# A batch's first layer as one full-precision product instead of three rounded ones, the gate of a convolution in one operation, and a new order

## The chip, the core and the metric

The kernel runs on one core of a Trainium2 chip. A core has a matrix engine (TensorE, PE in the profile; its weight loads are listed as PEld), three engines for elementwise work (VectorE or DVE, ScalarE or ACT, GpSimd or POOL), and SyncE (SP), whose queue issues nearly all of this program's DMAs. Each engine works through its own instructions in the order in which the program lists them, and engines wait for each other by semaphores. Operands lie in an on-chip memory of 128 partitions (SBUF); PE writes its products to eight accumulator banks (PSUM). The metric is the device time of one execution in microseconds.

## The reference, cut to what matters

```python
B, H, S, D = 4, 8, 576, 64                 # batches, heads, positions, head size
def attention(q, k, v):                    # windowed: 32 keys back; heads 4 to 7 with a step of 4
    scores = where(mask[h], q @ k.T / sqrt(D), -1e9)
    return softmax(scores) @ v             # joined over heads: x, (B, S, 512)

def gated_mlp(x, w_in, conv_w, w_out):     # w_in (512, 1024), w_out (1024, 512)
    h = maximum(x @ w_in, 0)               # the first layer
    conv = conv_w[0] * h[s - 1] + conv_w[1] * h[s] + conv_w[2] * h[s + 1]   # over positions
    return (h * sigmoid(conv)) @ w_out     # the second layer

def mixing(x, w_ch1, w_ch2):               # w_ch1 (512, 2048), w_ch2 (2048, 512)
    u = x + real(fft(fft(x, axis=1), axis=2))
    return u + maximum(normalize(u) @ w_ch1, 0) @ w_ch2
```

The weights arrive as 64-bit floats, and everything is wanted in 32-bit precision.

## The kernel before

**Precision by parts.** A product whose operands are rounded to a shorter mantissa (type fp32r in the listing) is one pass on PE. `mm3` makes a product of nearly full precision out of three: each operand is split into a high part (rounded) and a low part (the remainder), and high x high, high x low and low x high are added up in one bank. A split is a rounding copy on ScalarE or GpSimd and a subtraction (`lo_of`) on DVE. `mm` with plain fp32 operands is a full-precision product; the attention scores and the products with the values use it. In a trace a full fp32 product stands as two records.

**Stages.** The attention of a batch comes as 14 ticks (`tick`): scores by PE, a maximum over the keys by a GpSimd reduction, a subtraction on DVE, an exponential on ScalarE, the product with the values, a normalization, and a turn on PE that brings the result to x's layout (`xT[b]`: 128 partitions by four chunks of 576 positions, with a high and a low part). Batch b's gated MLP runs while the ticks of batch b + 1 are worked off. It goes over eight blocks of 128 features: `m1(b, f)` multiplies the first layer (two halves of 288 positions, four chunks, three passes: twelve products a half), takes ReLU into a padded row buffer `hpad`, makes the three taps of the convolution, tanh and the gate, and splits the gated result into `gh` and `gl`; `m2(b, f)` multiplies it by the second layer into banks 4 to 7 (four groups of three products of 512 columns). The gate is made in two operations, since the second half of the positions is stored back to front. After eight blocks `evac` copies the sums out and `fold` adds and subtracts mirrored positions for the Fourier transform, whose tables and products (`dft`), the normalization (`ln`) and the last MLP follow and take the rest of the time.

**Weights.** `Weights.convert` brings one tile of 128 x 512 raw 64-bit weights by DMA into one of two buffers (`raw`). Three integer operations on DVE (`narrow`) turn it into fp32 in place, and `split` makes the two parts that `mm3` needs. First-layer tiles (`W1.tiles[0, f]`) and second-layer tiles (`W1.tiles[1, f]`) of the gated MLP are made during batch 0 and stay for all four batches.

**What sets the order.** Nothing is issued while the code is recorded. `Plan` notes each operation with its reads, writes, an estimated duration per engine that may take it, and a due time. `order` then plays the engines forward and takes for each the ready work that is due first. Due times come from `T0`, `PER` (the period of a batch) and `WHEN`; `urgency` carries them back to what a work needs, and `NUDGES`, a list of random seeds, shifts the due times of works in random stretches of the plan. Where the plan finds PE idle for more than 0.4 us, `fill` puts in products of the identity matrix (`busy_with`, line 1277), called fillers here, which compute nothing that is used.

## Time and profile before

| | us |
|---|---|
| median of 3 runs | 738.28 |
| lowest, highest | 736.79, 740.48 |
| the profiled execution | 739.48 |
| its span, first instruction to last | 737.7 |

The profile is that of one execution. A row of a group gives how many instructions of one kind ran, how long they kept their engine, the mean duration of one, and the engine's idle time before them with what ended it. Products on PE overlap: the duration of one is longer than the distance from its start to the next one's start, so prices for PE are read from starts in the listing by time. In that listing (rows 5) consecutive equal products are merged into one row. Stages are cut here where PE starts the first product of a batch's first layer: at 40.0, 111.8, 189.3 and 248.4 us.

### The profile page before, as it was taken

How to read it: one execution, taken by the hardware profiler on the slowest of the kernel's cores; microseconds unless marked ns; L12 is line 12 of the kernel's file. 1: busy time of each engine (PE TensorE's matmuls, PEld its weight loads, DVE VectorE, ACT ScalarE, POOL GpSimd, SP SyncE). 2: the span in 40 equal slices, each digit the busy share in tenths (PEclk: the TensorE clock that was granted, in tenths of full speed). 3: DMA queues.
4: the chain of work that ended last, by engine and by line, in shares of the span. 5: the costliest groups of instructions: out<-in, count | busy, mean ns of one | idle time of the engine just before them, and what ended most of it. 6: DMA issues, size and time to landing. Idle time of an engine off the chain costs nothing.

```text
span 737.7 us, 12036 instructions
## 1 busy us (share of the span) xinstructions
PE 723.6 (98%) x4264; PEld 641.2 (87%) x4264; DVE 558.1 (76%) x1157; ACT 342.7 (46%) x874; POOL 156.5 (21%) x171
## 2 busy tenths in 40 slices
PE   7999999999999999999999999999999999999997
PEld 5888889998999999888798888898889889888896
DVE  5899999999998689999887988676788648324223
ACT  3876767776676665454333325233333323222211
POOL 5766425542554122120100100000010000000000
PEclk9999999999999999999999999999999999999999
DMA  8754444324600825687976813034456799546202
GB/s 284 236 170 129 157 133 154 118 79 133 205 23 1 282 88 185 203 297 244 342 242 203 283 57 115 29 142 129 143 185 235 244 366 367 150 121 228 87 1 87
DMA packets 75184, 126.85 MB, mean 172 GB/s; under 512 B 7594, under 2 KB 36010, under 8 KB 74484
## 3 DMA queue, kind: packets, MB, share of 16 engines
q1 hardware_dynamic: 74324, 123.13, 50.9%
q0 software_dynamic: 432, 2.67, 1.1%
q8 instruction: 34, 0.56, 0.3%
q10 hardware_dynamic: 368, 0.28, 0.1%
q14 instruction: 26, 0.21, 0.1%
HBM read 90.11 MB, written 35.94 MB: 171 GB/s over the span
## 4 chain that ended last, share of the span: by engine, by line
PE 84%; DVE 8%; DMA 4%; POOL 1%; issue 1%; SPq 1%; ACT 0%; ACTq 0%; DVEq 0%; POOLq 0%
PE pb L274 84%; DVE win L261 2%; DMA raw<-in_wm_dram 2%; DVE rows L261 2%; DVE wf L261 1%; POOL mx L261 1%; DMA unt<-nd 1%; DVE raw L261 1%; DMA cst<-in_conv_dram 1%; SPq L307 1%; DVE sm L261 1%; DMA maskt<-in_mask_dram 1%; DVE x L261 0%; POOL wf L261 0%; DVE hid L261 0%
## 5 line engine op out<-in xcount | busy, mean ns | idle before, releaser
L274 PE MATMUL pb<-wf,hid 128*128 128x512 f32 x870 | 229.8, 398 | 0.0
L274 PEld LDWEIGHTS pb<-wf,hid 128*128 128x128 f32 x870 | 157.0, 188 | 25.8 <-DVE hid L261 0.3
L274 PE MATMUL pb<-x,wf 128*128 128x288 f32 x768 | 116.1, 299 | 1.7 <-DVE wf L261 1.5
L274 PEld LDWEIGHTS pb<-x,wf 128*128 128x128 f32 x768 | 106.2, 188 | 4.9 <-DVE wf L261 2.5
L261 POOL PARTITION_ALL_REDUCE mx<-sm x56 | 86.5, 1558 | 59.7 <-DVE sm L261 28.4
L274 PE MATMUL pb<-wf,wc 128*128 128x384 f32 (+1 forms) x414 | 85.3, 343 | 0.0
L274 PEld LDWEIGHTS pb<-wf,wc 128*128 128x128 f32 x414 | 74.2, 188 | 6.0
L261 DVE TENSOR_TENSOR work<-pb,work 128x384 f32<-128x384 f32 x48 | 26.6, 555 | 64.0 <-ACT work L261 35.6
L261 ACT COPY work<-pb 128x384 f32<-128x384 f32 x48 | 23.0, 479 | 82.9 <-PE pb L274 82.9
L261 DVE SCALAR_TENSOR_TENSOR rows<-rows,convw 128x576 f32<-128x576 f32 x64 | 55.8, 872 | 3.6 <-ACT rows L261 2.9
L274 PE MATMUL pb<-wf 128*128 128x512 f32 x216 | 55.3, 393 | 0.0
L274 PEld LDWEIGHTS pb<-wf 128*128 128x128 f32 x216 | 40.1, 188 | 6.5
L673 ACT ACTIVATE xb<-pb,rs 72x64 f32<-72x64 f32 (+1 forms) x184 | 41.6, 305 | 7.8 <-DVE rs L261 7.7
L274 PEld LDWEIGHTS pb<-VT,sm 104*72 104x72 f32 (+1 forms) x448 | 39.4, 153 | 4.7 <-ACT sm L261 2.6
L274 PE MATMUL pb<-VT,sm 104*72 104x65 f32 (+1 forms) x448 | 41.2, 236 | 1.5 <-ACT sm L261 1.4
L274 PE MATMUL pb<-QT,KT 128*104 128x144 f32 (+1 forms) x224 | 41.0, 305 | 0.7 <-DMA QT<-in_qt_dram 0.7
L274 PE MATMUL pb<-wf,wf 128*128 128x512 f32 (+1 forms) x162 | 40.3, 385 | 0.0
L261 ACT ACTIVATE rows<-pb 128x288 f32<-128x288 f32 x64 | 26.5, 414 | 28.2 <-PE pb L274 27.9
L274 PEld LDWEIGHTS pb<-QT,KT 128*104 128x104 f32 (+1 forms) x224 | 33.2, 178 | 5.8 <-issue 3.8
L261 ACT ACTIVATE hid<-pb 128x512 fp32r<-128x512 f32 (+1 forms) x32 | 18.3, 572 | 35.9 <-PE pb L274 35.9
L274 PEld LDWEIGHTS pb<-wf,wf 128*128 128x128 f32 x162 | 30.0, 188 | 5.7
L274 PE MATMUL pb<-unt,wc 128*128 128x384 f32 x168 | 33.1, 335 | 0.0
(197 smaller groups left out, 1238.3 us busy)
## 6 DMA issues: line engine op xcount, KB each, us to landing
raw<-in_wm_dram SPq DMA_DIRECT2D x42, 512.0 KB, 4.9
wc<-cd SPq DMA_DIRECT2D x56, 256.0 KB, 3.5
cd<-wc SPq DMA_DIRECT2D x4, 1792.0 KB, 10.1
rows<-ud SPq DMA_DIRECT2D x20, 256.0 KB, 4.1
y<-yd SPq DMA_DIRECT2D x18, 256.0 KB, 4.3
ud<-y SPq DMA_DIRECT2D x18, 256.0 KB, 4.1
wf<-nd SPq DMA_DIRECT2D x18, 256.0 KB, 4.6
QT<-in_qt_dram SPq DMA_DIRECT2D x31, 144.0 KB, 3.5
```

Of the source, the lines that this page charges most:

```text
L261: getattr(self.engines[eng], name)(**a)
L274: getattr(self.engines["PE"], name)(*[v.real() for v in a], **kw)
L307: self.engines[eng].dma_start(out=out.real() if outs else out, in_=in_.real() if ins else in_)
L673: nc.scalar.mul(out=x[:, i], in_=p[:, i], mul=r[:, i:i + 1])
```

## The change

Batch 0's x is kept in fp32 alone (`x_first`, in space that the results of a batch use later), so a tick of batch 0 ends in one copy on ScalarE or DVE and no subtraction. Its first layer is multiplied by `mm` in full fp32: four products a half instead of twelve. For that the first-layer weights stay unsplit at first. `narrow` writes them to a small buffer (`ways`: three of them, in `e9` and `fs_t`), and a DMA brings them to their place; `later` splits them in place, block by block, when batch 1's turn comes. Each half now takes 290 columns instead of 288, two beyond its border, so that both halves lie in the row buffer with their own borders, the second one back to front from the start. The taps then run over both halves in one pattern of 2 x 289 elements, and the gate is one operation. A copy of one element sets the position that both halves share. The results of a batch (`y_t`, `o_t`, `e9`) become parts of one tile. `PER` and `NUDGES` change, and with them the order of the whole program.

```diff
-PER = 69.0
+PER = 68.0
-NUDGES = (8271, 49756, 57394, 51589, 33461, 98847, 32710, 84961, 42106, 40158, 90060, 79165,
+NUDGES = (55523, 99683, 99992, 79439, 80785, 13914, 19249, 38109, 26493, 77070, 73723, 9275,
...
-    rows_t = moe.tile([128, 4 * (S + 2)], F32, "rows")
-    hpad = [rows_t[:, i * (S + 2):(i + 1) * (S + 2)] for i in range(2)]
-    cv_t, g_t = (rows_t[:, i * (S + 2):i * (S + 2) + S] for i in (2, 3))
+    HW, GW = HS + 3, HS + 1
+    rows_t = moe.tile([128, 4 * HW + 4 * GW], F32, "rows")
+    hpad = [rows_t[:, 2 * HW * i:2 * HW * (i + 1)] for i in range(2)]
+    cv_t, g_t = (rows_t[:, 4 * HW + 2 * GW * i:4 * HW + 2 * GW * (i + 1)] for i in range(2))
...
-    y_t = [low.tile([128, DM], F32, "y") for _ in range(4)]
-    o_t = low.tile([128, DM], F32, "o")
-    e9 = low.tile([128, DM], F32, "e9")
+    y6 = low.tile([128, 6 * DM], F32, "y")
+    *y_t, o_t, e9 = (y6[:, DM * i:DM * i + DM] for i in range(6))
+
+    x_first = y6[:, 0:4 * S].rearrange("p (c s) -> p c s", c=4)
...
+    ways = Ring([e9, fs_t[:, 0:512].bitcast(F32), fs_t[:, 512:1024].bitcast(F32)])
...
             if load:
                 dma(raw, self.src[f, :, i])
-            self.split(w, raw)
+            if self.late and not i:
+                way = ways()
+                self.narrow(raw, way)
+                dma(w[:, 0].bitcast(F32), way)
+            else:
+                self.split(w, raw)
...
+        def later(self, f):
+
+            w = self.tiles[0, f]
+            w0 = w[:, 0].bitcast(F32)
+            copy(w[:, 1], w0, ("ACT", "POOL"))
+            lo_of(w[:, 0], w0, w[:, 1])
+            self.tiles[0, f] = w[:, 1::-1]
...
         x = xT[b][:, hp]
+        if not b:
+            x = x_first[:, hp]
+            if dil:
+                x = x.rearrange("p (m r) -> p m r", r=4)[:, :, t]
+            else:
+                x = x[:, 192 * t:192 * t + 192]
+            P.run({"ACT": 0.41 if dil else 0.32, "DVE": 0.42 if dil else 0.35}, "copy", at + 10, out=x, in_=bt)
+            return
...
+        def taps(at, row):
+            return rows_t[:, h0 + at:h0 + at + 2 * row].rearrange("p (t s) -> p t s", t=2)[:, :, :GW]
         for half in range(2):
-            o = of("h", h_banks)[:, :HS]
-            sl = slice(HS * half, HS * half + HS)
+            o = of("h", h_banks)[:, :HS + 2]
+            sl = slice(286 * half, 286 * half + HS + 2)
             with P.products(at + 4.3 * half):
                 for c in range(4):
                     wsl = slice(128 * c, 128 * c + 128)
-                    mm3(o, w[:, 0, wsl], w[:, 1, wsl], xT[b][:, c, 0, sl], xT[b][:, c, 1, sl], c == 0, c == 3)
-            P.run({"ACT": 0.41}, "activation", out=hp[:, 1 + HS * half:1 + HS * half + HS], in_=o, func=AF.Relu,
-                  scale=0.5)
...
+                    if b:
+                        mm3(o, w[:, 0, wsl], w[:, 1, wsl], xT[b][:, c, 0, sl], xT[b][:, c, 1, sl], c == 0, c == 3)
+                    else:
+                        mm(o, w[:, 0, wsl].bitcast(F32), x_first[:, c, sl], c == 0, c == 3)
+            P.run({"ACT": 0.41}, "activation", out=hp[:, HW + 2:] if half else hp[:, 1:HW],
+                  in_=o[:, HS + 1:0:-1] if half else o, func=AF.Relu, scale=0.5)
...
-        dve("scalar_tensor_tensor", 0.48, out=g[:, 0:289], in0=cv[:, 0:289], scalar=1.0, in1=hp[:, 1:290],
-            op0=ALU.add, op1=ALU.mult)
-        dve("scalar_tensor_tensor", 0.48, out=g[:, 289:576], in0=cv[:, 575:288:-1], scalar=1.0,
-            in1=hp[:, 576:289:-1], op0=ALU.add, op1=ALU.mult)
+        dve("scalar_tensor_tensor", 0.77, out=g, in0=cv, scalar=1.0, in1=taps(1, HW), op0=ALU.add, op1=ALU.mult)
+        P.run({"ACT": 0.2, "POOL": 0.3}, "copy", out=g[:, 1, 0:1], in_=g[:, 0, HS:GW])
...
             at = T0 + PER * b + step * f
+            if b == 1:
+                W1.later(f)
             m1(b, f, h_banks, at)
```

What the order becomes is shown at three places. In the listings `pb0` to `pb7` are the banks, a row with x12 stands for twelve equal instructions.

PE in batch 0's stage, before, from one half of feature block 1 to the next block's (`x_192` is batch 0's x, `wf4_152` the first-layer weights of blocks 0 to 3, `QT`/`KT` the scores, `VT` the product with the values, `ident`/`xb` the turn):

```order
L274 MATMUL pb0_134<-QT_203,KT_200 128x192 x2
L274 MATMUL pb2_136<-x_192,wf4_152 128x288 x12
L274 MATMUL pb3_137<-ident_145,xb_220 128x96 x2
L1277 LDWEIGHTS ident_145
L1277 MATMUL pb4_138<-ident_145 128x256
L274 MATMUL pb1_135<-VT_206,sm_210 96x65 x4
L274 MATMUL pb2_136<-x_192,wf4_152 128x288 x12
```

The same place after (`y_177` holds `x_first`):

```order
L273 MATMUL pb2_136<-y_177,wf4_152 128x290 x4
L273 LDWEIGHTS ident16_192
L273 MATMUL pb0_134<-maskt_191,ident16_192 128x384
L273 MATMUL pb0_134<-QT_198,KT_195 128x192 x2
L273 MATMUL pb2_136<-y_177,wf4_152 128x290 x4
L273 MATMUL pb1_135<-VT_201,sm_205 96x65 x4
L273 LDWEIGHTS ident16_192
L273 MATMUL pb0_134<-maskt_191,ident16_192 104x288
L273 MATMUL pb0_134<-QT_196,KT_193 104x144 x2
L273 MATMUL pb2_136<-y_177,wf4_152 128x290 x4
```

Twelve products became four, the filler is gone, and a tick's scores stand in its place; over the whole program there were 75 fillers and are 13 (six at the program's start, two more ahead of batch 0's first product, none in the stages of the MLP's first three batches, five later).

DVE around batch 0's first convolution (`rows<-rows,convw`), before: a first-layer weight tile is split right there (`wf4_152`), then a second-layer tile is narrowed (`win`, `raw`) and split (`wf_155`).

```order
L261 TENSOR_TENSOR wf4_152<-raw_161,wf4_152 128x512
L261 RECIPROCAL rs_216<-rs_216 96x4
L261 TENSOR_SCALAR win_163<-raw_162 128x512
L261 SCALAR_TENSOR_TENSOR win_163<-raw_162,win_163 128x512
L261 SCALAR_TENSOR_TENSOR raw_162<-raw_162,win_163 128x512
L261 SCALAR_TENSOR_TENSOR rows_169<-rows_169,convw_146 128x576 x2
L261 TENSOR_TENSOR x_167<-pb7_141,x_167 128x192
L261 RECIPROCAL rs_217<-rs_217 96x4
L261 TENSOR_TENSOR wf_155<-raw_162,wf_155 128x512
```

After:

```order
L260 TENSOR_TENSOR wf_155<-raw_162,wf_155 128x512
L260 TENSOR_TENSOR x_167<-pb6_140,x_167 128x192
L260 TENSOR_SCALAR win_163<-raw_161 128x512
L260 SCALAR_TENSOR_TENSOR win_163<-raw_161,win_163 128x512
L260 TENSOR_TENSOR x_167<-pb7_141,x_167 128x192
L260 SCALAR_TENSOR_TENSOR rows_169<-rows_169,convw_146 128x578 x2
L260 TENSOR_TENSOR x_167<-pb1_135,x_167 128x192
L260 SCALAR_TENSOR_TENSOR y_177<-raw_161,win_163 128x512
L260 SCALAR_TENSOR_TENSOR rows_169<-rows_169 128x578
```

The first-layer tile that is narrowed here (block 3's, into `y_177`, which is `e9`) has no split; the gate is one row (`rows_169<-rows_169 128x578`). Between the first convolutions of batch 0 and batch 1 DVE has 13 splits before and 8 after.

DVE around batch 0's last convolution, shortly before PE can reach batch 1's first product, after (`wf4_152<-wf4_152` is a split by `later`, `x_167` a low part of batch 1's x; the last of these stands in the third row):

```order
L260 TENSOR_TENSOR wf4_152<-wf4_152 128x512
L260 RECIPROCAL rs_211<-rs_211 96x4
L260 TENSOR_TENSOR x_167<-pb3_137,x_167 128x144
L260 TENSOR_TENSOR hid_168<-rows_169,hid_168 128x2x288
L260 TENSOR_TENSOR wf_157<-raw_161,wf_157 128x512
L260 TENSOR_TENSOR sm_206<-sm_206,mx_209 128x384
L260 SCALAR_TENSOR_TENSOR rows_169<-rows_169,convw_146 128x578 x2
L260 TENSOR_TENSOR x_187<-pb1_135,x_187 128x192
L260 TENSOR_TENSOR wf4_152<-wf4_152 128x512
```

The splits of batch 1's first-layer weights are new in this place; the first two blocks' stand around the last convolution of batch 0 (the row with x2), six follow after batch 1's first convolution.

## Rows read from the trace of the kernel before

**Rows 1.** By stage: us; busy (x instructions): PE, PEld, DVE, ACT, POOL; clock; DMA:

```profile
20.00:40.00 20.00, 18.51 (x188) 16.77 (x188) 18.14 (x52) 16.71 (x62) 16.20 (x12) 1.00 0.68 210
40.00:111.80 71.80, 68.03 (x500) 60.73 (x498) 70.29 (x130) 50.38 (x154) 34.64 (x32) 1.00 0.45 146
111.80:189.30 77.50, 77.50 (x533) 70.72 (x532) 71.99 (x144) 53.87 (x153) 33.21 (x33) 1.00 0.38 123
...
248.40:737.70 489.30, 484.63 (x2514) 426.61 (x2512) 336.23 (x702) 171.64 (x354) 33.06 (x52) 1.00 0.56 185
```

**Rows 2.** The same stretches, filler products (line 1277) alone: PE and PEld:

```profile
20.00:40.00 20.00, 2.79 (x21) 1.98 (x21) 1.00 0.68 210
40.00:111.80 71.80, 4.87 (x37) 3.53 (x37) 1.00 0.45 146
...
248.40:737.70 489.30, 1.37 (x11) 1.00 (x11) 1.00 0.56 185
```

**Rows 3.** PE groups, batch 0's stage: count | busy us, mean ns | idle:

```profile
L274 PE MATMUL pb<-x,wf 128*128 128x288 f32 x192 | 30.4, 303 | 1.7 <-DVE wf L261 1.5
L274 PE MATMUL pb<-wf,hid 128*128 128x512 f32 x72 | 20.2, 408 | 0.0
...
L274 PE MATMUL pb<-QT,KT 128*128 128x192 f32 x20 | 4.2, 331 | 0.0
```

**Rows 4.** The same in batch 1's stage, 111.8 to 189.3 us:

```profile
L274 PE MATMUL pb<-wf,hid 128*128 128x512 f32 x120 | 33.3, 406 | 0.0
...
L274 PE MATMUL pb<-wf,g 128*128 128x512 f32 x24 | 5.8, 391 | 0.0
L274 PE MATMUL pb<-QT,KT 128*128 128x192 f32 x26 | 5.5, 330 | 0.0
```

**Rows 5.** PE in order of time: start us, us, what, x records:

```profile
127.00 0.81 PE L274 MATMUL pb<-QT,KT 128*128 128x192 f32 x4
127.65 0.33 PE L274 MATMUL pb<-ident,xb 96*128 96x96 f32 x2
...
142.65 1.76 PE L274 MATMUL pb<-x,wf 128*128 128x288 f32 x12
144.25 0.85 PE L274 MATMUL pb<-wf,hid 128*128 128x512 f32 x3
144.94 0.65 PE L274 MATMUL pb<-QT,KT 128*104 128x144 f32 x4
145.43 0.29 PE L274 MATMUL pb<-ident,xb 72*128 72x72 f32 x2
...
191.62 0.87 PE L274 MATMUL pb<-QT,KT 128*128 128x192 f32 x4
192.32 0.33 PE L274 MATMUL pb<-ident,xb 96*128 96x96 f32 x2
```

**Rows 6.** PE's waits, 20 to 112 us: total us, times, longest:

```profile
PE pb L274 <- DVE wf L261: 1.5, 3, 0.9
PE pb L274 <- ACT sm L261: 1.4, 3, 0.5
```

**Rows 7.** DVE groups, batch 0's first convolution to batch 1's (46.6:123):

```profile
L261 DVE SCALAR_TENSOR_TENSOR rows<-rows,convw 128x576 f32<-128x576 f32 x16 | 14.2, 889 | 0.1
...
L261 DVE TENSOR_TENSOR wf<-raw,wf 128x512 fp32r<-128x512 f32 x13 | 10.2, 799 | 0.0
...
L261 DVE SCALAR_TENSOR_TENSOR rows<-rows 128x287 f32<-128x287 f32 x8 | 4.7, 590 | 0.0
L261 DVE SCALAR_TENSOR_TENSOR rows<-rows 128x289 f32<-128x289 f32 x8 | 4.2, 528 | 0.1
```

**Rows 8.** DMA issues of the page: count, KB each, us to landing:

```profile
rows<-ud SPq DMA_DIRECT2D x20, 256.0 KB, 4.1
```

**Rows 9.** A small GpSimd operation, groups of 0 to 60 us:

```profile
L261 POOL CAST g<-hid 128x64 fp32r<-128x64 f32 x2 | 0.9, 440 | 0.1
```

**Rows 10.** The program's first products, PE groups of 0 to 20 us:

```profile
L274 PE MATMUL pb<-sm 128*128 128x512 bf16 x11 | 4.9, 632 | 1.4 <-DVE sm L254 1.4
```

More of the change, by code (lines that the diff above doesn't have):

```diff
@@ L189 @@
     __slots__ = ("where", "fn", "deps", "key", "bytes", "after", "start", "eng", "left", "ready", "succ", "id")
-NUDGES = (8271, 49756, 57394, 51589, 33461, 98847, 32710, 84961, 42106, 40158, 90060, 79165,
-          93730, 5245, 20901, 71335, 68800, 25156, 21360, 86375, 72590, 67213, 53755, 27334,
-          86850, 19207, 89900, 19196, 38517, 50276, 48044, 21112, 6820, 15954,)
+NUDGES = (55523, 99683, 99992, 79439, 80785, 13914, 19249, 38109, 26493, 77070, 73723, 9275,
+          56440, 18534, 69082, 2124, 89064, 50742, 31974, 73006, 19128,)
 LAT = {"PE": 0.25, "DVE": 0.12, "ACT": 0.15, "POOL": 0.2, "SP": 0.0, "NO": 0.0}
@@ L560, in tile_kernel, with __init__ @@
     class Weights:
-        def __init__(self, src, n, lead):
-            self.src = src
+        def __init__(self, src, n, lead, late=False):
+            self.src, self.late = src, late
             self.todo = sorted([(f + lead * i, i, f) for f in range(n) for i in range(2)])
@@ L581, in split, with narrow @@
             lo_of(w[:, 1], w0, w[:, 0])
-        def narrow(self, raw):
+        def later(self, f):
[4 more added lines that the diff above has]
+            self.tiles[0, f] = w[:, 1::-1]
+        def narrow(self, raw, to=None):
             wv = raw.bitcast(I32).rearrange("p (n t) -> p n t", t=2)
@@ L590, in narrow @@
                 op0=ALU.bitwise_and, op1=ALU.bitwise_or)
-            dve("scalar_tensor_tensor", 0.7, out=w0.bitcast(U32), in0=w0.bitcast(U32), scalar=29,
+            to = w0 if to is None else to
+            dve("scalar_tensor_tensor", 0.7, out=to.bitcast(U32), in0=w0.bitcast(U32), scalar=29,
                 in1=win.bitcast(U32), op0=ALU.logical_shift_right, op1=ALU.bitwise_or)
-            return w0.bitcast(F32)
-    W1 = Weights(wm1, NF1, 2)
+            return to.bitcast(F32)
+    W1 = Weights(wm1, NF1, 2, True)
     W2 = Weights(wm2, NF2, 0.9)
@@ L714, in m1 @@
         w = W1.tiles[0, f]
+        h0 = 2 * HW * (s % 2)
         hp = hpad[s % 2]
+        def taps(at, row):
+            return rows_t[:, h0 + at:h0 + at + 2 * row].rearrange("p (t s) -> p t s", t=2)[:, :, :GW]
         for half in range(2):
-            o = of("h", h_banks)[:, :HS]
-            sl = slice(HS * half, HS * half + HS)
+            o = of("h", h_banks)[:, :HS + 2]
+            sl = slice(286 * half, 286 * half + HS + 2)
             with P.products(at + 4.3 * half):
@@ L721, in m1 @@
                     wsl = slice(128 * c, 128 * c + 128)
-                    mm3(o, w[:, 0, wsl], w[:, 1, wsl], xT[b][:, c, 0, sl], xT[b][:, c, 1, sl], c == 0, c == 3)
-            P.run({"ACT": 0.41}, "activation", out=hp[:, 1 + HS * half:1 + HS * half + HS], in_=o, func=AF.Relu,
-                  scale=0.5)
-        cv, g = cv_t, g_t
-        P.run({"ACT": 0.78}, "mul", out=cv, in_=hp[:, 1:S + 1], mul=convw[:, NF1 + f:NF1 + f + 1])
-        dve("scalar_tensor_tensor", 0.86, out=cv, in0=hp[:, 0:S], scalar=convw[:, f:f + 1], in1=cv,
+                    if b:
[4 more added lines that the diff above has]
+                  in_=o[:, HS + 1:0:-1] if half else o, func=AF.Relu, scale=0.5)
+        cv, g = (v.rearrange("p (t s) -> p t s", t=2) for v in (cv_t, g_t))
+        P.run({"ACT": 0.78}, "mul", out=cv, in_=taps(1, HW), mul=convw[:, NF1 + f:NF1 + f + 1])
+        dve("scalar_tensor_tensor", 0.86, out=cv, in0=taps(0, HW + 2), scalar=convw[:, f:f + 1], in1=cv,
             op0=ALU.mult, op1=ALU.add)
-        dve("scalar_tensor_tensor", 0.88, out=cv, in0=hp[:, 2:S + 2],
+        dve("scalar_tensor_tensor", 0.88, out=cv, in0=taps(2, HW - 2),
             scalar=convw[:, 2 * NF1 + f:2 * NF1 + f + 1], in1=cv, op0=ALU.mult, op1=ALU.add)
         P.run({"ACT": 0.69}, "activation", out=cv, in_=cv, func=AF.Tanh)
-        dve("scalar_tensor_tensor", 0.48, out=g[:, 0:289], in0=cv[:, 0:289], scalar=1.0, in1=hp[:, 1:290],
-            op0=ALU.add, op1=ALU.mult)
-        dve("scalar_tensor_tensor", 0.48, out=g[:, 289:576], in0=cv[:, 575:288:-1], scalar=1.0,
-            in1=hp[:, 576:289:-1], op0=ALU.add, op1=ALU.mult)
+        dve("scalar_tensor_tensor", 0.77, out=g, in0=cv, scalar=1.0, in1=taps(1, HW), op0=ALU.add, op1=ALU.mult)
+        P.run({"ACT": 0.2, "POOL": 0.3}, "copy", out=g[:, 1, 0:1], in_=g[:, 0, HS:GW])
         gh, gl = hid[s] = gh_t[s % 2], gl_t[s % 2]
-        gs = g.rearrange("p (t s) -> p t s", t=2)
+        gs = g[:, :, :HS]
         copy(gh, gs, ("ACT", "POOL"))
@@ L1324, in tile_kernel @@
         dve("memset", 0.05, out=t[:, 0:1])
-        dve("memset", 0.05, out=t[:, S + 1:S + 2])
+        dve("memset", 0.05, out=t[:, HW:HW + 2])
     dve("memset", 0.3, out=fo)
-    dve("memset", 0.3, out=e9)
     conv_load()
@@ L1371, in tile_kernel @@
         W1.convert(place[i, f], raws[k % 2], k > 1)
+    dve("memset", 0.3, out=e9)
     for b in range(3):
```

## The prediction

> **What bounds the kernel now.** I read the busy time by stage first, cutting the span where TensorE (PE) starts the first product of a batch's first layer: 40.0, 111.8, 189.3 and 248.4 us. In batch 1's stage PE is busy 77.50 of 77.50 us, and in the long rest 484.63 of 489.30 [rows 1]; there only less work on PE makes the program shorter. Batch 0's stage is different: PE 68.03 of 71.80, VectorE (DVE) 70.29 of 71.80 [rows 1]. PE waits there, and of what it does 4.87 us are 37 products of the identity that fill planned gaps and compute nothing [rows 2].
>
> How much of batch 0's stage is lost? The next stage is full, so it serves as the price list: the two stages hold the same first-layer products and the same ticks but for these. Batch 1 has 120 + 24 second-layer products against 72 [rows 3, 4], and three of them take 144.94 - 144.25 = 0.69 us [rows 5], so 72 less are 16.6 us. It has 26 against 20 records of 192-column scores [rows 3, 4], four to 0.65 us [rows 5]: 1.0 us less. Batch 0's has some ten mask products of a filler's size, 0.13 us each [rows 2]: 1.3 us more. 77.5 - 16.6 - 1.0 + 1.3 = 61.2 us of work; with 4.9 of fillers, 71.8 - 66.1 = **5.7 us of waiting** remain. The waits name DVE's weight tiles first, then ScalarE's exponentials [rows 6]. So DVE sets this stage, and 5.7 + 4.9 = 10.6 us are the most that a relief of DVE can give there.
>
> **The change part by part.**
>
> Full fp32 products. Per half of a feature block 12 products of 288 columns become 4 of 290. Twelve take 144.25 - 142.65 = 1.60 us [rows 5]. No row has a full fp32 product of this size; the attention scores are the nearest. Two of 192 columns (four records) take 127.65 - 127.00 = 0.65, two of 144 take 145.43 - 144.94 = 0.49 [rows 5]: 0.325 and 0.245 each, so 1.67 ns a column, and 0.325 + 98 x 1.67 ns = 0.49 for 290. Four are 1.95. 16 halves x (1.95 - 1.60) = 5.6 us more. The dear end is a pair that took 192.32 - 191.62 = 0.70 [rows 5]: 0.35 x 290/192 = 0.53, four 2.11, so +8.2. The cheap end keeps 1.95 but lets twelve cost the stage's busy share, 30.4/192 = 0.158 each and 1.90 in all [rows 3]: +0.8. A gain is excluded: a column costs 1.67 ns against three times 0.133/288, 1.39 ns. I take +4.8, near the rows of a full stretch, with a little for what twelve lose at their ends.
>
> The Trainium skill (TensorE: Matmul & The Clock Gate, Back-to-back issue gap) gives N/2.4 + 2.5 ns for a product alone, 122.5 ns for 288 columns; twelve would be 1.47 us as an estimate, and the change would then cost 7.7 us with the 1.95 above. The row of twelve, 0.133 each, decides against it here: these products alternate with weight loads.
>
> 290 columns in batches 1 to 3: 576 products with 2 columns more, a quarter of 1.67 ns each: +0.5 us.
>
> DVE in batch 0. No low parts of x are subtracted, and the eight splits of first-layer weights move behind batch 0's use. The build's order puts 8 splits instead of 13 between batch 0's first convolution and batch 1's: 5 x 0.80 = 4.0 us less [rows 7]. The gate's two operations, 0.528 + 0.590, become one of 578 elements, like a tap at 0.889 [rows 7]: 0.23 less, 1.8 in eight blocks; at the worst it costs the sum, no gain. Some attention steps moved ahead of the stage, about 3 us by count. So DVE needs about 70.3 - 8.8 = 61.5 us, where PE needs 61.2 + 4.8 = 66.0. PE is late next. But DVE keeps about nine tenths of the stage, and PE runs in order: a late turn or exponential still holds it. I leave 2.5 of the 5.7 us of waiting and take -3.2 (from 0 to -5.7).
>
> Fillers. The build has 13 instead of 75. In batch 0's stage all 37 are gone: -4.9 us, since the work behind them is there earlier. Of the 21 between 20 and 40 us (2.79 us [rows 2]) two are left. They covered the chain of the last ticks, which does not get shorter by less DVE work alone; but GpSimd's reductions of ticks 14 and 15 no longer stand behind a weight cast. I take -1.2 of 2.5. The rest of the program loses six of eleven, 0.12 each [rows 2]: -0.7.
>
> Costs that I set to nothing. The low parts of the first layer's weights come back in batch 1: six splits at 0.80 in its stage, less 1.8 for the gates, so DVE goes from 71.99 to about 75.0 of 77.5 [rows 1, 7]; it fits, by 2.5 us (the first rival). Each batch-0 weight now goes through a DMA on SP's queue, which waits for DVE's narrowing; keys, queries and raw weights are queued behind it. A transfer of that size lands 4.1 us after its issue [rows 8]; the narrowing stands three blocks, over 20 us, ahead of the product. With that cover gone it would be 4 us once. The one-element copy behind the gate has no row; the nearest is GpSimd's 64-element cast, 0.44 us [rows 9]. It lies on ScalarE or GpSimd, busy 50.4 and 34.6 of 71.8 [rows 1], behind a buffer of two blocks; uncovered, 3.5 us a batch.
>
> **Sum.** +4.8 + 0.5 - 3.2 - 4.9 - 1.2 - 0.7 = -4.7 us. The profiled execution took 739.48 (span 737.7), so it would be 734.8; it lies 1.2 above the median, and against that median the forecast is 738.3 - 4.7 = **733.6 us**.
>
> **Rivals.**
>
> *The handover to batch 1.* In the build's order the split of batch 1's first tile and the last low part of its x stand on DVE around batch 0's last convolution, close ahead of the time at which PE can reach batch 1's first product. If DVE arrives late, PE stands still there, and in a stage with 2.5 us to spare on DVE it does not catch up. For it: DVE's 75 of 77.5. Against it: the lag of DVE behind PE at that place shrinks by what batch 0 saves. It takes back some 2.5 us: 736.1.
>
> *All waiting goes.* DVE's relief frees the last 2.5 us and the early fillers' 1.3: 729.8. For it: DVE has 4.5 us less work than PE there. Against: the exponentials' share of the waits [rows 6].
>
> *Slower: PE's waits are not DVE's.* If batch 0's stage is held by the ticks' chain (scores, reduction, exponential, products, turn), then bare waiting takes the place of each filler, and the fp32 products come on top: +4.8 + 0.5 - 0.7 = +4.6, 742.9. The point: of 13.1 us in waits and fillers up to the end of batch 0's stage (5.7 + 4.9 + 2.5) PE must win back 4.6 to break even. For it: ScalarE's exponentials end 1.4 us of the recorded waits, DVE's weight tiles 1.5 [rows 6], and GpSimd's reductions are unchanged. Against it: DVE's 98% in this stage.
>
> *The clock.* In all stretches of rows 1 the granted clock is 1.00, the level of 2.4 GHz. At the program's start 512 columns take 4.9/11 = 0.45 us [rows 10] against 0.23 later [rows 5], the other level. Without fillers PE would sit idle in gaps; should the clock fall for a stretch of 10 us, that work costs 10 us more: 743.6. Against it: the longest wait recorded between 20 and 112 us is 0.9 [rows 6], with the clock at 1.00. The Trainium skill (TensorE: Matmul & The Clock Gate, HAM oscillation — how this bites in real kernels) says that idle gaps between products send the array back to half rate; the trace of before has none long enough to show it.
>
> *Not what it says.* The build shows the 64 full products and 13 fillers; little is left of this.
>
> **How the numbers follow.** Forecast 0.52 (731 to 736), handover 0.22, all waiting gone 0.15, slower chain 0.08, clock 0.03. The range leaves out the two slow rivals (0.11) and the far ends of the others. It takes in the forecast with the dear end of fp32 (+3.4: 737.0) and with the cheap end (-4.0: 729.6), and the handover with half of that dear end added: 729.5 to 739.0. About 0.5% (3.7 us), what a measurement of this kernel can tell from no change, puts the bounds at 734.6 and 742.0. Faster: three quarters of the forecast, the good rival and a little of the handover, 0.57; slower 0.10; same 0.33.
>
> **What would show it.** Full fp32 products of 290 columns: eight records (four products) in 1.95 us. PE's work between the first products of batch 0 and batch 1: some 68.5 us long instead of 71.8, no fillers, DVE under 95%. The first product of batch 0 at about 39, of batch 1 at about 107. Batch 1's stage still 77 to 78 us; if it is 80 or more, the handover rival holds. Waits of PE named by ScalarE in batch 0 of over 6 us would show the slower rival. The granted clock must read 1.00 in 20 to 112 us. The forecast is wrong if the fp32 group takes over 2.2 us, or if the later order, from 248 us on, moves by more than 2 us in either direction.

## The result, and the profile after

The changed kernel takes **732.53 us** (median of 5 runs, 731.59 to 733.23) against 738.28 before: a ratio of 0.9918, 95% interval 0.9896 to 0.9940. That is 5.75 us, 0.8%, faster; 733.6 was forecast. The profiled execution took 731.86 us with a span of 729.7.

The stages of after, cut as in [rows 1] (us; busy with the number of instructions of PE, PEld, DVE, ACT, POOL; clock; DMA). Batches start at 36.06, 103.10, 180.57 and 242.09:

```profile
20.00:36.06 16.06, 15.79 (x161) 14.55 (x160) 14.86 (x42) 13.48 (x49) 13.89 (x11) 1.00 0.88 286
36.06:103.10 67.04, 66.73 (x391) 54.46 (x391) 64.89 (x117) 51.44 (x157) 37.61 (x39) 1.00 0.56 178
103.10:180.57 77.47, 77.47 (x529) 70.42 (x528) 72.71 (x135) 51.37 (x153) 41.74 (x43) 1.00 0.38 124
180.57:242.09 61.52, 60.72 (x448) 56.34 (x447) 52.28 (x105) 43.51 (x137) 31.28 (x33) 1.00 0.31 92
242.09:729.70 487.61, 483.36 (x2505) 425.86 (x2503) 336.73 (x689) 172.46 (x359) 36.49 (x57) 1.00 0.57 187
```

Fillers in the same stretches, as in [rows 2] (line 1308 now):

```profile
20.00:36.06 16.06, 0.38 (x2) 0.16 (x2) 1.00 0.88 286
36.06:103.10 67.04, 0.00 (x0) 0.00 (x0) 1.00 0.56 178
...
242.09:729.70 487.61, 0.72 (x5) 0.41 (x5) 1.00 0.57 187
```

Batch 0's stage went from 71.8 to 67.04 us. PE is busy in all of it but 0.3 us and has no fillers; before, 4.87 us of fillers and 3.8 us of idle time stood in it. But DVE is busy 64.89 of 67.04 as well: **two engines fill this stage**, and the next line names the one wait of PE (us in all, times, longest) that is recorded from 20 to 112 us. [Rows 6] shows 2.9 us in two rows; three smaller ones (0.8, 0.7 and 0.2 us) bring before's to 4.6:

```profile
PE pb L273 <- DVE x L260: 0.2, 1, 0.2
```

Batch 1's stage kept its 77.5 us. The first product of batch 0 comes 3.95 us earlier. Batch 2's stage is 2.4 us longer (59.15 before, its row stands below under later work) and the rest 1.7 shorter. Together the span lost 8.0 us and the execution 7.6 (739.48 to 731.86); the medians differ by 5.75, because before's execution lies 1.2 above its median and after's 0.7 below.

The new products, PE in order of time (start, duration, x records):

```profile
42.42 2.22 PE L273 MATMUL pb<-y,wf 128*128 128x290 f32 x8
44.48 0.33 PE L273 MATMUL pb<-maskt,ident 128*128 128x384 bf16 x1
...
45.29 2.12 PE L273 MATMUL pb<-y,wf 128*128 128x290 f32 x8
47.24 0.81 PE L273 MATMUL pb<-VT,sm 128*96 128x65 f32 x8
```

From start to next start four products (eight records) take 2.06 and 1.95 us, where the prediction has 1.95. Of all sixteen groups thirteen take 1.95 to 2.06; the others take 1.74, 1.79 and 2.25.

DVE's groups from batch 0's first convolution to batch 1's (43.7 to 110.5), to be read beside [rows 7]:

```profile
L260 DVE SCALAR_TENSOR_TENSOR rows<-rows,convw 128x578 f32<-128x578 f32 x16 | 15.4, 965 | 0.2
...
L260 DVE SCALAR_TENSOR_TENSOR rows<-rows 128x578 f32<-128x578 f32 x8 | 6.3, 786 | 0.1
...
L260 DVE TENSOR_TENSOR wf<-raw,wf 128x512 fp32r<-128x512 f32 x6 | 4.1, 690 | 0.6 <-POOL wf L260 0.6
...
L260 DVE TENSOR_TENSOR wf<-wf 128x512 fp32r<-128x512 f32 x2 | 1.6, 783 | 0.0
```

Eight splits instead of 13, as the order showed; the gate is one operation of 0.786. The taps, which nobody meant to change, went from 889 to 965 ns in the mean. Their median went only from 811 to 821; what raises the mean is in the last section.

### The profile page after: what moved, and what is told of

The parts are those of the page before. It is cut to its first block, busy times and chain, and to the rows that moved or that the text cites. A ratio compares the mean times of both kernels' runs of the same rounds, so it can differ in the third digit from the quotient of the medians.

```text
span 729.7 us, 11752 instructions
## 1 busy us (share of the span) xinstructions
PE 720.3 (99%) x4138; PEld 634.3 (87%) x4138; DVE 552.9 (76%) x1117; ACT 341.8 (47%) x876; POOL 172.6 (24%) x195
## 4 chain that ended last, share of the span: by engine, by line
PE 71%; DVE 1%; DMA 1%; POOL 0%; issue 0%; ACT 0%; SPq 0%; DVEq 0%; POOLq 0%
PE pb L273 71%; DMA work<-ud 1%; DVE sm L260 0%; POOL hid L260 0%; DVE rows L260 0%; DVE fo L260 0%; SPq L306 0%; DVE sq L260 0%; DVE fs L260 0%; DVE st L260 0%; DVE hid L260 0%; DVE wf L260 0%; ACT wf L260 0%; PE pb L1308 0%; POOL mx L260 0%
## 5 line engine op out<-in xcount | busy, mean ns | idle before, releaser
L260 POOL PARTITION_ALL_REDUCE mx<-sm x56 | 81.7, 1481 | 49.1 <-DVE sm L260 21.2
L273 PE MATMUL pb<-x,wf 128*128 128x290 f32 x576 | 86.5, 299 | 0.0
L273 PEld LDWEIGHTS pb<-x,wf 128*128 128x128 f32 x576 | 81.0, 189 | 2.5
L260 DVE TENSOR_TENSOR work<-pb,work 128x384 f32<-128x384 f32 x48 | 26.7, 556 | 69.9 <-ACT work L260 38.6
L260 DVE SCALAR_TENSOR_TENSOR rows<-rows,convw 128x578 f32<-128x578 f32 x64 | 58.4, 912 | 2.6 <-ACT rows L260 1.8
L260 ACT ACTIVATE rows<-pb 128x290 f32<-128x290 f32 x64 | 26.5, 414 | 26.7 <-PE pb L273 26.1
L260 POOL CAST g<-hid 128x64 fp32r<-128x64 f32 x46 | 27.7, 607 | 38.9 <-ACT hid L260 29.2
L260 POOL CAST wc<-raw 128x512 fp32r<-128x512 f32 (+1 forms) x10 | 6.7, 668 | 123.8 <-PE pb L273 65.5
```

The source lines that it names most:

```text
L260: getattr(self.engines[eng], name)(**a)
L273: getattr(self.engines["PE"], name)(*[v.real() for v in a], **kw)
```

## The experiments

The theory was the prediction's: before the change DVE alone holds batch 0's stage, and PE is late next behind it. Twelve kernels tell its parts from their rivals. Each is before (`b_`) or after (`a_`) with one edit; but for the two plain ones the order of the other instructions is their parent's.

**More work on DVE, in both kernels.** One narrowing step (0.73 us) is issued twice in eight tiles, 5.9 us in all. The edit is the same in both:

```diff
-                op0=ALU.bitwise_and, op1=ALU.bitwise_or)
+                op0=ALU.bitwise_and, op1=ALU.bitwise_or, times=2 if self.src is wm1 and raw is raws[0] else 1)
```

> The kernel before, its order unchanged, with 8 more operations on VectorE while weights are narrowed: one step of every second tile is issued twice (0.73 us each, 5.9 us in all, 6 or 7 of them in batch 0's stage); the outputs stay the same. Theory (VectorE sets batch 0's stage in the kernel before): nearly all of it shows, +4 to +6 us, 742.5 to 744. Rival (the ticks' chain or the order sets the stage, VectorE has room): 0 to +1.5 us, 738 to 740.

> The changed kernel, its order unchanged, with the same 8 more operations on VectorE (5.9 us). Theory A (TensorE alone sets batch 0's stage now, VectorE has some 4.5 us of room there): +0 to +2 us on the changed kernel's 732.5, so 732.5 to 734.5. Rival (VectorE, busy 64.9 of 67.05 us in that stage, sets it together with TensorE): +3.5 to +6 us, 736 to 738.5.

Measured: before with it 743.68 us (741.24 to 744.73), after with it 738.01 (735.79 to 739.79): 5.4 and 5.5 us more. The two stages, before's first:

```profile
41.33:117.02 75.69, 69.11 (x500) 60.46 (x499) 74.22 (x137) 49.96 (x153) 33.76 (x32) 1.00 0.45 139
38.55:109.85 71.30, 67.81 (x391) 54.53 (x391) 69.48 (x123) 50.42 (x156) 37.83 (x39) 1.00 0.55 167
```

Seven of the eight extra operations stand in before's stage (DVE has 137 instructions there instead of 130) and six in after's (123 instead of 117): 5.1 and 4.4 us. The stages grew by 3.9 and 4.3 us, while PE's work stayed. So DVE holds the stage in before, as the prediction read it, and it still does in after. "PE is late next, with DVE having room" falls. The rest of the growth in the medians is less sure: in both profiles DVE also waited 2.4 us for a small transfer at the start (below), and before's has 3.4 us at the half clock there.

**More work on PE, in both kernels.** Repeated products of batch 0's first layer, whose result the next product overwrites: 64 rounded ones in before (8.5 us by 0.133 each), 16 full ones in after (7.8 us by 0.49 each). The edit of after is shown; before's issues its first rounded product four more times a half in the same way.

```diff
             with P.products(at + 4.3 * half):
+                if not b:
+                    P.piece += [(0.0, "matmul", (o, w[:, 0, 0:128].bitcast(F32), x_first[:, 0, sl]),
+                                 dict(start=True, stop=False, skip_group_check=True))]
                 for c in range(4):
```

> The kernel before, its order unchanged, with more work on TensorE in batch 0's first layer: the first product of each half is issued four more times (64 products of 288 columns at 0.133 us, 8.5 us; outputs unchanged). Theory (TensorE waits 5.7 us in that stage, for VectorE): the waits take up 4 to 5.7 us of it, so +2.8 to +4.5 us, 741 to 743. Rival (TensorE sets the stage, the time that is not its own is not free): +7 to +8.5 us, 745 to 747.

> The changed kernel, its order unchanged, with one more full fp32 product of 290 columns a half in batch 0's first layer (16 at an expected 0.49 us, 7.8 us; outputs unchanged). Theory (TensorE sets the stage): all of it, +7 to +8.5 us on 732.5, so 739.5 to 741. Rival (VectorE sets it as much): some of it is hidden in TensorE's waits, +3 to +6 us. The distance from the start of such a group of five to the next instruction should be 0.49 us longer than that of a group of four.

Measured: 739.5 (738.91 to 741.56), 1.2 us above before for 8.5 us of work; 739.63 (738.93 to 742.61), 7.1 above after for 7.8. The stages of the two in that order, and the groups of after with five products instead of four:

```profile
39.08:113.21 74.13, 74.08 (x565) 69.30 (x563) 68.81 (x131) 50.57 (x154) 35.54 (x33) 1.00 0.44 142
```

```profile
40.00:113.61 73.61, 73.61 (x424) 60.85 (x424) 65.65 (x117) 49.95 (x157) 35.56 (x39) 1.00 0.52 162
```

```profile
43.49 2.63 PE L273 MATMUL pb<-y,wf 128*128 128x290 f32 x10
45.96 0.81 PE L273 MATMUL pb<-VT,sm 128*96 128x65 f32 x8
```

In before the stage grew by 74.13 - 71.82 = 2.3: 6.2 of the 8.5 us went into waiting that was there already, near the 5.7 that the prediction worked out. In after it grew by 6.6 of 7.8: about a microsecond of room. Five products take 2.47 in this row and 2.44 in most of the sixteen groups, where four take 1.95, so one is 0.49, as forecast.

**Less work on PE.** The fourth of the four full products of each half is left out (batch 0's hidden values are incomplete by it):

```diff
-                        mm(o, w[:, 0, wsl].bitcast(F32), x_first[:, c, sl], c == 0, c == 3)
+                        mm(o, w[:, 0, wsl].bitcast(F32), x_first[:, c, sl], c == 0, c == 2)
+                        if c == 3:
+                            us, _, ops, kw = P.piece.pop()
+                            P.piece.append((us, None, ops, kw))
```

> The kernel after, without the fourth of the four full fp32 products of each half in batch 0's first layer (16 products of 0.49 us, 7.8 us of TensorE's work; that part of the sum is left out, so batch 0's hidden tiles are incomplete). Everything else stands in its order. If TensorE alone set batch 0's stage after the change, the stage falls by most of 7.8 us and the time is about 725 to 727 us. If VectorE, which was busy 64.9 of the stage's 67.05 us, sets it with TensorE, the stage can fall by no more than some 2 us and the time is 729.5 to 732 us, with TensorE then waiting for VectorE's and ScalarE's tiles again. I expect the second, 730.5 us.

Measured: 732.23 (730.8 to 735.18), no gain that can be told, where the second theory expected 729.5 to 732. Its stage, and the first of PE's waits in it (us in all, times, longest):

```profile
37.63:103.91 66.28, 61.05 (x359) 48.35 (x359) 64.55 (x116) 49.24 (x155) 36.67 (x39) 1.00 0.59 181
```

```profile
PE pb L274 <- DVE x L260: 2.4, 3, 1.0
PE pb L274 <- DMA wf<-fs: 1.0, 1, 1.0
PE pb L274 <- ACT rows L260: 0.6, 1, 0.6
...
```

PE had 7.8 us less to do and the stage lost 0.8. Most of the rest came back as waits: PE idles 5.2 us in this stage, 5.1 of it in recorded waits, against 0.3 in after. With the loads above this closes the question: PE and DVE hold the stage of after together. A dearer full product would have moved the end by nearly its own size, a cheaper one would not. The second name is new: PE waited once, 1.0 us, for the DMA that brings a narrowed weight tile to its place, the cover that the prediction took as whole. In after, with PE's full work, no such wait is recorded.

**Fillers.** The 75 fillers of before are left out:

```diff
-    P.busy_with = busy_with
```

> The kernel before without its 75 fillers (9.0 us of TensorE's time, 37 of them in batch 0's stage), all other instructions in their order. The fillers compute nothing and stand where the plan saw TensorE wait. If they lie in real gaps, bare waiting takes their place: 737 to 739 us with the granted clock at 1.00. If they were on the path in batch 0's stage, part of the prediction's 4.9 us shows here alone: 733 to 736 us. If they hold the clock up (the prediction's clock rival), some stretch shows a granted clock of 0.5 and the time is 742 us or more. I expect the first, 737.5 us.

Measured: 739.37 (736.77 to 743.19), the ratio to before 1.0008 (0.9983 to 1.0033). A short stretch ahead of batch 0's stage and that stage, and three rows of PE around the start of the first:

```profile
34.48:41.30 6.82, 5.89 (x36) 5.63 (x35) 6.46 (x15) 4.80 (x16) 4.96 (x4) 0.50 0.74 226
41.20:111.82 70.62, 64.03 (x463) 57.45 (x462) 69.14 (x127) 49.38 (x151) 33.10 (x32) 1.00 0.46 147
```

```profile
34.08 0.32 PE L274 MATMUL pb<-ident,xb 72*128 72x72 f32 x2 [1.22 <-DVE xb L670]
...
36.84 1.54 PE L274 MATMUL pb<-VT,sm 128*96 128x65 f32 x8 [0.93 <-ACT sm L261]
...
40.01 1.43 PE L274 MATMUL pb<-VT,sm 128*96 128x65 f32 x8
```

Two things are seen. The stage is only 1.2 us shorter without its 4.87 us of fillers: most of their time turned into waiting. And for 6.8 us the granted clock is 0.50, the level of 1.2 GHz: eight records (four products) with the values take 1.43 us there, and 0.81 to 0.89 at 1.00. PE had just waited 1.22 us, where before put fillers. The mean granted clock was 0.988 to 0.998 in the ten executions of this kernel, and 0.998 to 1.0 in 17 of the 19 of before beside them. So the fillers did hold the clock up in most executions, at a price of some 1 us in the stage, and the two sides cancel in the time: the three executions without fillers that kept a mean clock of 0.998 took 736.77 to 737.5, below before's median of 738.28, and the slowest two, at 0.988 and 0.993, 743.19 and 742.52. The expectation came near the time (737 to 739) and had the clock wrong.

**The stretch ahead of batch 0's first product.** First the copies of batch 0's tokens are made twice; then a GpSimd cast is put behind the reductions of ticks 13 and 15, near where before had weight casts.

```diff
-            P.run({"ACT": 0.41 if dil else 0.32, "DVE": 0.42 if dil else 0.35}, "copy", at + 10, out=x, in_=bt)
+            P.run({"ACT": 0.41 if dil else 0.32, "DVE": 0.42 if dil else 0.35}, "copy", at + 10, times=2, out=x, in_=bt)
```

> The kernel after, with each copy of a piece of batch 0's tokens issued twice (8 more on VectorE of about 0.38 us = 3.0 us, 6 more on ScalarE of about 0.33 us = 2.0 us), which puts back on these two engines about what the removed low parts took before batch 0's first product. The prediction's early term says that this load was hidden by the ticks' chain for about half: the first product of batch 0 then comes 1 to 1.5 us later (37 to 40 us instead of 36 to 38.5) and the time is 733.5 to 734 us. Rival one: nothing of it was on the path, the time stays at 732.5 and the early gain came from the other changes (GpSimd's casts, order). Rival two: all of VectorE's 3.0 us is on the path, 735.5 us.

```diff
+        if n in (13, 15):
+            def reduced(_):
...
+                nc.gpsimd.tensor_copy(out=place[1, 7][:nk, 0, :w].real(), in_=sm.real())
+            P.add({"POOL": 1.5}, reduced, [sm], [mx])
+        else:
```

> The kernel after, with one more cast of 384 columns on GpSimd behind the reductions of ticks 13 and 15, where the kernel before had casts of weight pieces between the reductions. If GpSimd's chain of reductions sets when batch 0's first product can start, the two casts (about 0.5 to 1.1 us each) delay it by 1 to 2 us and the time is 733.5 to 734.5 us. If the reductions have room, nothing changes: 732 to 733 us. I expect the first at 733.5 us, with less certainty than for the runs before.

Measured: 736.02 (734.98 to 736.25) with the copies, 3.5 us more; in the one of its five executions that had a mean clock of 1.000 it is 2.5 (734.98), and the profiled one has 3.4 us at the half clock among the first ticks. So the time is nearest to the second rival, by which all of DVE's extra copies stand on the path. But the edit also doubles ScalarE's copies, and the run does not part the two engines. With the casts 734.42 (732.31 to 735.67), 1.9 more. GpSimd in order of time in before, after and the kernel with the casts. Tick 13's reduction is the last of the three in before's first row (it starts at 29.73), the first of the six in after, and the first row with the casts:

```profile
26.61 4.34 POOL L261 PARTITION_ALL_REDUCE mx<-sm  x3
30.83 1.26 POOL L261 CAST wf<-raw 128x512 fp32r<-128x512 f32 x1
32.07 1.41 POOL L261 PARTITION_ALL_REDUCE mx<-sm  x1
35.44 2.24 POOL L261 PARTITION_ALL_REDUCE mx<-sm  x1 [1.97 <-ACT sm L261]
```

```profile
28.66 9.00 POOL L260 PARTITION_ALL_REDUCE mx<-sm  x6 [0.56 <-ACT sm L260]
```

```profile
30.25 1.15 POOL L673 PARTITION_ALL_REDUCE mx<-sm  x1 [0.55 <-ACT sm L260]
31.28 0.82 POOL L675 CAST wf<-sm 104x288 fp32r<-104x288 f32 x1
32.08 1.41 POOL L260 PARTITION_ALL_REDUCE mx<-sm  x1
33.39 1.50 POOL L673 PARTITION_ALL_REDUCE mx<-sm  x1
```

From the start of tick 13's reduction (29.73, 28.66, 30.25) to batch 0's first product (40.01, 36.06, 37.89) it is 10.28 us in before, 7.40 in after and 7.64 with the casts; with the double copies it is 31.58 to 40.58, 9.00. Other executions of the two orders gave 10.28 to 10.31 and 7.40 to 7.41. So this stretch really lost 2.9 us. The two casts give back 0.24 of it, the copies 1.6. Most of the rest lies ahead of tick 13 in its profile (30.25 against 28.66), where its edit has no part, and is the variation of the next run. So the time fell into the range that was expected of the casts, but by chance.

**A wait at the start.** In several profiles DVE waits for the small transfer of the convolution's constants, with the first ticks' subtractions queued behind it. It was 1.4 us in before, 0.3 in after, 1.0 and 1.4 in the two runs above, 2.4 in both with DVE's load. That transfer is issued ahead of four loads (a pair of query halves counted as one):

```diff
-        for w in self.order():
+        todo = self.order()
+        w = todo.pop([x.id for x in todo].index(self.soon.id))
+        at = [i for i, x in enumerate(todo) if x.bytes and x.eng == "SP"][9]
+        for w in todo[:at] + [w] + todo[at:]:
...
-        dma(st, conv_w)
+        P.soon = dma(st, conv_w)
```

> The kernel after, with the small transfer of the convolution's constants issued ahead of four of the transfers that stood before it on SyncE; nothing else moves. VectorE's queue waited for that transfer between 14 and 16.5 us, 0.3 to 2.4 us in the six profiles so far, with the first attention ticks' subtractions queued behind it, and batch 0's first product came between 36.1 and 41.3 us. If that wait is on the path, it is gone in every execution, the first product comes at about 36 to 37 us and the time falls by 0.5 to 1.5 us to 731 to 732 us, with a smaller spread. Rival: the key and value loads of the next ticks come late instead and the time is 732.5 to 733.5 us.

Measured: 731.7 (731.32 to 732.83). DVE's waits from 8 to 40 us, with the edit:

```profile
DVE sm L260 <- POOL mx L260: 6.8, 3, 5.1
DVE rs L260 <- ACT rs L260: 0.2, 1, 0.2
```

The wait is gone from its profile, and this is the lowest median of all; but 0.8 us below after is within what the runs' intervals leave open (ratio to before 0.9912, 0.9897 to 0.9927).

**The gate.** It is made in two operations of 289 again:

```diff
-        dve("scalar_tensor_tensor", 0.77, out=g, in0=cv, scalar=1.0, in1=taps(1, HW), op0=ALU.add, op1=ALU.mult)
+        hm = taps(1, HW)
+        def gate(_):
+            for t in range(2):
+                nc.vector.scalar_tensor_tensor(out=g[:, t].real(), in0=cv[:, t].real(), scalar=1.0, in1=hm[:, t].real(),
+                                               op0=ALU.add, op1=ALU.mult)
+        P.add({"DVE": 0.77}, gate, [cv, hm], [g])
```

> The kernel after with the gate made in two operations of 289 elements again; nothing else changes. By the rows of before two such operations take 0.53 + 0.59 us, the one takes 0.79 in the profile after: 0.33 us more on VectorE in each block, 2.6 us in batch 0's eight blocks, where VectorE sets the stage with TensorE, and in other stages behind TensorE. If that holds, the time is 734 to 735.5 us; if the gate lies on no path, it stays at 732 to 733. I expect 734.5 us.

Measured: 732.28 (731.0 to 732.98), no difference. DVE's group from 43.7 to 110.5 us:

```profile
L769 DVE SCALAR_TENSOR_TENSOR rows<-rows 128x289 f32<-128x289 f32 x16 | 6.8, 467 | 0.1
```

Two means of 0.467 make 0.93 a block, but the two operations overlap: sixteen keep DVE busy for 6.8 us, where after's eight of 0.786 take 6.3. That is 0.5 us in eight blocks, not the 2.6 that I expected. The means of before, from which the 0.33 a block came, hold operations that ran slowly beside GpSimd (last section). The stage of this profile is 0.9 us longer (67.93), but the gate does not show in it: all work on the row buffers keeps DVE busy for 25.21 us there and for 25.46 in after. So the one-operation gate by itself is worth about half a microsecond.

**Arithmetic or order.** Both kernels in the order that the planner makes without its table of numbers:

```diff
-PER = 68.0
+PER = 69.0
...
+NUDGES = ()
```

> The kernel after in the order that the planner makes without its table of numbers and with the period of before (69): the new arithmetic without the new order. Together with the next run (the kernel before in that same way) it tells what the arithmetic alone brings. If the gain of 5.7 us lies in the arithmetic (VectorE relieved in batch 0), the two plain kernels differ by 4 to 8 us in its favour; if it lies in the order that was chosen for it, they differ by less than 2 us. I expect both slower than their parents by 5 to 15 us and a difference of 5 us.

> The kernel before in the order that the planner makes without its table of numbers, with its own period of 69. The other half of the comparison with the run before this one: 743 to 754 us, and 4 to 8 us above it if the arithmetic makes the gain, within 2 us of it if the order does.

Measured: 740.93 (739.57 to 744.91) and 747.81 (745.52 to 748.69). The new arithmetic is 6.9 us faster in the plain order and 5.75 in the tuned ones; the tables (in after with its period of 68) bring 8.4 us in after and 9.5 in before. Batch 0's stages of the two, after's arithmetic first:

```profile
35.39:105.19 69.80, 67.83 (x398) 54.73 (x396) 64.02 (x117) 48.98 (x152) 36.26 (x38) 1.00 0.57 183
```

```profile
39.11:112.93 73.82, 67.32 (x494) 60.72 (x494) 69.81 (x130) 49.34 (x149) 30.77 (x28) 0.98 0.46 149
```

The stage is 4.0 us shorter (before's lies with 3.4 us at the half clock, so a little less), its start 3.7 earlier: the same two places as in the tuned pair (4.8 and 3.95). So the gain belongs to the arithmetic, and the new table adds none to it, as far as one order of each can tell.

Where each load or relief went, from the profiles (us; the stretch runs from tick 13's reduction to batch 0's first product, the stage from there to batch 1's):

| kernel | median | stretch | batch 0's stage |
|---|---|---|---|
| before | 738.28 | 10.28 | 71.82 |
| + 5.9 on DVE | 743.68 | 10.31 | 75.69 |
| + 8.5 on PE | 739.5 | 10.28 | 74.13 |
| - fillers | 739.37 | 11.64 | 70.62 |
| after | 732.53 | 7.40 | 67.04 |
| + 5.9 on DVE | 738.01 | 7.41 | 71.30 |
| + 7.8 on PE | 739.63 | 7.40 | 73.61 |
| - 7.8 on PE | 732.23 | 7.40 | 66.28 |
| + copies of x | 736.02 | 9.00 | 67.23 |
| + two casts | 734.42 | 7.64 | 67.79 |
| constants earlier | 731.7 | 7.41 | 67.27 |
| gate in two | 732.28 | 7.41 | 67.93 |

## Why the prediction came out, step by step

The time lies 1.1 us below the forecast, inside its range. The terms are not all right: two errors of opposite sign meet.

| term of the sum | predicted | in the profiles | what showed it |
|---|---|---|---|
| batch 0's stage: fp32 +4.8, waits -3.2, fillers -4.9 | -3.3 | -4.8 | the stage's rows |
| stretch ahead of it | -1.2 | -2.9 (from tick 13 on) | 10.28 to 7.40 us |
| batch 1's stage | 0 | 0.0 | 77.5 in both |
| batch 2's stage and the rest: fillers -0.7, 290 columns +0.5 | -0.2 | +2.2 | 59.15 to 61.52; the rest below |
| sum | -4.7 | -5.5 | medians: -5.75 |

**DVE sets batch 0's stage before.** Shown: 5.1 us on DVE in this stage made it 3.9 longer, 8.5 us on PE 2.3; the medians grew by 5.4 and 1.2. The waiting worked out from the next stage as a price list, 5.7 us, is what the load on PE found (6.2).

**Full fp32 at 1.95 a group.** Right: 1.95 to 2.06 us in thirteen of sixteen groups, taken from the columns of the attention's scores. Groups of twelve took 1.59 to 1.79 in before's stage where no wait fell into them, 1.68 in the mean, so the surcharge is 16 x (1.95 - 1.68) = 4.3 us, near the +4.8.

**Waits -3.2: mis-sized, and for a wrong reason.** The prediction left 2.5 us of waiting above 61.2 + 4.8 = 66.0 us of work, because PE runs in order, and gave DVE 61.5 us, 4.5 under PE. Measured are 67.04 us for the stage, so about 1.0 was left, and DVE at 64.89, 97% where under 95% was said. DVE's relief of 8.8 us was 5.4. Compare the groups of DVE within the stage: the splits gave 3.9 of their 4.0 us (12 to 8, 9.6 to 5.7 us) and the gate its 1.8, but the taps took 1.2 back (14 from 901 to 986 ns), and the 3 us of attention steps "by count" did not leave; 0.9 us in other steps did. The gate's 1.8 is luck in part: made of two operations it took only 0.5 more in after. Its means and those of the taps hang on which of them ran beside a reduction of GpSimd. That PE still waits so little with DVE at 97% means that the two queues fit each other, not that DVE has room; leaving out a quarter of the full products showed it.

**Fillers -4.9: right only together with the waits.** Taken alone out of before they bring 1.2 us in the stage. They go in after because the work behind them is ready earlier, as the prediction says, and what makes it ready is DVE's relief, with waits and fillers counted as one account of 10.6 us: 5.7 + 4.9 there, 1.0 left. The 9.6 us paid for 4.8 of dearer products.

**Early fillers -1.2: mis-sized.** 2.9 us went between tick 13 and the first product. The prediction held that the last ticks' chain "does not get shorter by less DVE work alone" and put its hope in GpSimd's casts. It is the other way round: the casts are worth 0.24 in the run that put them back, the copies of x 1.6 in this stretch, on DVE and ScalarE together; the 2.5 to 3.5 by which their run is longer hold the variation of the start as well. What else took part, above all the splits of 1.30 and 1.22 us that stand among the last ticks on DVE's queue in before, was not tried alone. A further 1.1 us of the 3.95 in the two profiles lies ahead of tick 13 and is no work of the change: another execution of before's order started tick 13's reduction at 28.80, after at 28.66.

**Later work -0.2: a miss.** Batch 2's stage got longer by 2.4 us. Before's row of it, and the one wait of PE in after's:

```profile
189.26:248.41 59.15, 59.05 (x443) 54.77 (x441) 50.69 (x107) 41.63 (x133) 28.92 (x31) 1.00 0.32 103
```

```profile
PE pb L273 <- ACT sm L260: 0.8, 1, 0.8
```

After's stage holds two more records of scores and four more second-layer products, 0.33 and 0.92 by [rows 5], and PE idles 0.8 us in it where 0.1 stood. Both kernels in the plain order have 61.33 us there with the new arithmetic and 62.24 with the old, so the 2.4 go with the tuned order and not with the arithmetic. The rest of the program had 489.3 us in before's profile, but 487.5 to 488.0 in three kernels that share its order from there on, and 487.0 to 488.0 in after's family. So its 1.7 us are mostly that one execution's, and I count -0.2 there. Batch 1's stage has six records of scores fewer, 1.0 us, and did not get shorter; two more records of the turn, one more second-layer product and the 290 columns explain some 0.6 us of it, the rest is open.

**The rivals.** *Handover to batch 1:* fell; its first product followed without a recorded wait, the stage kept 77.5, and DVE was busy for 72.71 us of it, not the 75 that the rival rests on. *All waiting goes:* the nearest in mechanism. The stage lost 1.5 and the start 1.7 us more than the forecast, as this rival says; batch 2's stage kept its 729.8 from coming true. *Slower chain:* fell; no wait for ScalarE is recorded in batch 0's stage. *Clock:* its cause is real (the profile without fillers has the half clock), but it did not act in after: the granted clock is 1.00 in all five stretches. Two kernels in after's order did fall to it among the first ticks (last section), so after is not free of it. The rule of the Trainium skill that was named with it (TensorE: Matmul & The Clock Gate, HAM oscillation — how this bites in real kernels) agrees in its direction with the half clock behind the 1.22 us wait, which no run had shown when the prediction was made; the Trainium skill tells it there of long waits for DMA, and here a shorter wait for DVE stood ahead of it.

## What to carry to other kernels

When two engines each fill about 95% of a stage, price an edit by what it takes from both: work given from the one that holds the stage to the one that waits pays until they are level, and from there more or less work on either alone changes little for the better and everything for the worse. Count waits and planned fillers as one account, and don't expect the fillers' time from taking them out: they may be the cover that keeps the clock up. Test a new order by taking the tuning off both kernels; if the difference stays, it is the arithmetic's.

## What the runs showed of the hardware

**The start of the program varies by microseconds.** The same small transfer, issued in the same place, let DVE wait from 0.3 to 2.4 us over the profiles, or not at all, and most of what stands behind it moved along: batch 0's first product came between 35.8 and 38.6 us in the kernels that share after's order there, and at 40.0 in the one whose clock fell on top of it.

**The clock falls for short stretches.** In five of the fourteen profiles the granted clock was 0.50 for 3.4 to 6.8 us before the program's end: three times among the first ticks, once just ahead of batch 0's stage and once inside it. The kernel with more work on PE after the change, ahead of and in such a stretch:

```profile
11.00:18.31 7.31, 5.57 (x49) 5.17 (x47) 4.22 (x11) 4.30 (x14) 7.24 (x6) 1.00 1.03 329
...
18.31:25.14 6.83, 6.58 (x36) 6.43 (x37) 5.44 (x16) 3.88 (x14) 3.77 (x3) 0.50 0.45 144
```

Each fall came at or soon after a wait of PE for DVE: 1.58 us here and with the double copies, 2.25 in before with DVE's load, 1.22 without fillers, 1.83 in before's plain order. But waits of 1.58 at the same place in before and with the casts, and of 1.91 in after with DVE's load, passed at 1.00. So a wait of this size alone does not tell when the clock falls.

**A DVE operation took longer beside a reduction on GpSimd.** The taps around batch 0's stage in before and after (shortest, median and longest in ns), and three rows of after in order of time:

```profile
L261 DVE SCALAR_TENSOR_TENSOR rows<-rows,convw x16: 783/811/1223, 46.7 to 114.8; 128x576 f32<-128x576 f32 x16
L260 DVE SCALAR_TENSOR_TENSOR rows<-rows,convw x16: 787/821/1379, 43.8 to 104.6; 128x578 f32<-128x578 f32 x16
```

```profile
85.73 1.31 POOL L260 PARTITION_ALL_REDUCE mx<-sm  x1
...
85.95 1.22 DVE L260 SCALAR_TENSOR_TENSOR rows<-rows,convw 128x578 f32<-128x578 f32 x1
...
88.02 0.80 DVE L260 SCALAR_TENSOR_TENSOR rows<-rows,convw 128x578 f32<-128x578 f32 x1
```

Taps with no GpSimd work beside them took 0.78 to 0.82 us in both kernels. Taps beside a reduction for more than 0.9 us took 1.10 to 1.38. Shorter stretches beside it, and casts, cost some taps and others not, and the link was not tried alone. The form matters little: two runs of 289 columns cost 10 ns more than one of 576 by the median. Two gate operations in a row took 0.81 us from start to end back to front in before and 0.82 in the kernel with the split gate, one operation 0.75.
